# The fill of a tile of ones put first in a hand-ordered S4 + SwiGLU kernel, with a later planned start

## The chip, the cores and the metric

The kernel runs on one core of one Trainium2 chip. The metric is device time in microseconds (us) of one execution; smaller is better.

## The reference, cut to what matters

A layer norm feeds two branches, and their product is added to the input. L is 2048 rows, D 512 channels, N 128 states, F 1792.

```
x  = A_u                                   # 1 x 2048 x 512, float32
xn = layernorm(x)
P  = exp(dt * A * arange(L))               # complex, 512 x 128 x 2048
K  = real(einsum("dn,dnl,dn->dl", C, P, dt * B))
s  = causal_fft_convolution(xn, K) + xn * Dskip
g  = silu( (silu(xn @ w_gate) * (xn @ w_up)) @ w_down )
out = x + s * g
```

## The kernel before, in words

**What is computed where.** The feed-forward branch is done in float16 with a high and a low part of every operand, so that each product takes three matmuls (lines 699 and 741). The weights w_gate and w_up come in seven column chunks (g0 to g6, u0 to u6), each a load of 512 KB into a slot named wd. For each chunk ScalarE sums squares (line 604), VectorE copies the sums into hsq (line 614), one small TensorE matmul with a constant tile `ones` adds them over the partitions (line 615), VectorE makes the scale from that (lines 624 to 639), ScalarE writes the high part (line 669, L666 for u1 and later) and VectorE or GpSimd the low part (lines 670 and 667). The input rows x0 to x3 are loaded first (line 489), normed on VectorE and ScalarE (lines 503 to 531), transposed by TensorE (line 540) and copied back (line 546). Line 563 is the first stage of the convolution, whose results (line 567) are written to memory on SyncE's queue (line 568). Later come the convolution's kernel (lines 1070 to 1178), the products in frequency (1230 to 1287) and the output stage (1324 to 1340).

**What sets the order.** Every piece of work is a `Task` with an engine, a planned duration and its buffers. The string `LIST` (line 47) holds the order of all tasks, two characters for each; the first two tasks that the code adds, ids 0 and 1, are the fills

```
add("DVE", 0.2, lambda: (V.memset(ones, 2.0 ** -26), V.memset(halfpi, math.pi / 2)), up=[key("ones")], c=0)
add("POOL", 0.6, lambda: G.memset(dsk, 0.0), wr=[key("dsk")], c=0)
```

`ones` is read by line 615 and by the warming matmuls below; `halfpi` is read by ScalarE much later. Each engine issues its tasks in the order of the list. `Plan.run` walks through the list and gives every task a planned start and end, from its engine's free time, the ends of the tasks that it depends on plus a latency by engine (0.65 for PE, 0.35 for DVE and ACT), and a model of the transfers: `dma_free` is when the transfers planned so far are over, a transfer adds max(bytes / 280e3, pieces * 1.2e-3) us to it, and its data count as landed 1.9 us later. From the planned times come the PSUM bank of every task, the place of every buffer in the tile `arena` (`place`), extra waits that keep some VectorE and GpSimd work apart (`part_ports`), and the warming matmuls.

**The warming matmuls** (`keep_warm`, run at line 1423) are products of `ones` with itself into an unused bank; nobody reads them. For each planned gap of TensorE, from its end s of earlier work (1.5 for the first, `WARM_FROM`) to the planned start e of the next task, `keep_warm` puts

```
n = int((e - s - 0.2) * WARM_SHARE / WARM_DUR)      # 0.8 / 0.213
```

of them ahead of that task, if enough of the surrounding 3.4 us is idle in the plan. They do not alter the planned times of the tasks.

**Around the start**, the order on VectorE in the list before is: statistics of x1 and x0, the newton steps of their norm (lines 509 to 517), the hsq copy of g0, the fill of `ones` and `halfpi`, the low part of x0 (line 531), the scale of g0. The first TensorE task is the line 615 matmul of g0, with the first group of warming matmuls ahead of it.

Of the kernel before, what the change touches and what calls it, by code (L numbers as in the profile page):

```python
# [20 lines left out]
P = 128  # L21
L = 2048
D = 512
N = 128
# [20 lines left out]

DIGITS = "".join(chr(c) for c in range(35, 126) if c != 92)
LIST = (
    "#)#(#'#K#&#%#J#L#.#T#i#M#N#k###l#/#O#U#R#j#m#V#n#1#v#P#2#Q#S#D#Y#4#W#-#X#Z#5#+#w#o#x#y#q#,#p#r#*&+#8#z(*#s#t&.(+"
    "#]&/(,(.#}$&#7#[$'$(${(/$)#C#d#;#{#^&0#|$#(0#e(4#_#`&E#f%S&3$*#g&,#a$+#h#b#c(-#:$$(1$-#<&5$w&v(5$2&:&8$x(6$z$y$,"
    "#>$1$3$|$.(7&=#9%#$/(:(;$4$}#=&;#A(@&x$5$6$<%%%.$7&4$=$>(L$8(<%&(M&A$?$@$k$H$G$I(F(2#@(N$;%$(3&9#?$C&1&u#B$9(=&F"  # L50
    "%/(>%((H$D%2$J#0$K(?#6#3(G(I$:$A$S$R$T$N(O$L$B$t(A(R(S(B(J(K$E&6$F$O$](T$M(X(Z$q(P#E&J(C&@$%&?$Q(8(9(Q$0&y$P#u$U"
# [69 lines left out]
class Plan:  # L121
# [54 lines left out]

    def run(self):
        order = [self.tasks[i] for i in LIST]
        free = dict.fromkeys(("PE", "DVE", "ACT", "POOL", "SP"), 0.0)
        flight = {e: [] for e in free}  # L180
        banks = {k: [[None, 0.0] for _ in range(n)] for k, n in self.BANKS.items()}
        used, leaving, taken = 0, [], 0.0
        dma_free = port_free = 0.0
        shape = 0
        for at, t in enumerate(order):
            e, s = t.eng, free[t.eng]
            for d in t.deps:
                s = max(s, d.end + (0.0 if d.eng == e != "SP" else self.LAT[e]))
            for b in t.bufs:
                if b.over is not None:  # L190
                    continue
                b.over, b.first = 0.0, 2 * at
                if b.kind == "sb":
                    used += b.size
                    s = max(s, taken)
                    while used > ROOM and leaving:
                        x, n = heapq.heappop(leaving)
                        used -= n
                        s = max(s, x)
                    taken = s  # L200
                    continue
                best = None
                for k in b.kind:
                    for i, (held, x) in enumerate(banks[k]):
                        if held is None and (best is None or max(x, s) < best[0] - 1e-9):
                            best = max(x, s), k, i
                s, k, i = best
                b.at = k, i
                banks[k][i][0] = b
            if t.port:  # L210
                s = max(s, port_free)
            x = s + t.dur
            if e == "PE" and t.f32 != shape:
                x += SWITCH
                shape = t.f32
            t.start, free[e] = s, x
            if t.port:
                port_free = x
            if t.dma:
                dma_free = max(dma_free, x) + t.dma  # L220
                x = dma_free + 1.9
                flight[e].append(x)
                if len(flight[e]) >= 8:
                    free[e] = max(free[e], flight[e][-8])
            t.end = x
            for b in t.bufs:
                b.over = max(b.over, x)
                b.left -= 1
                if b.first == 2 * at:
                    b.since = round(s * 1e4)  # L230
                if not b.left:
                    b.till, b.last = round((b.over + REUSE) * 1e4), 2 * at + 1
                    if b.kind == "sb":
                        heapq.heappush(leaving, (b.over + REUSE, b.size))
                    else:
                        banks[b.at[0]][b.at[1]] = [None, b.over + REUSE]
        self.span = max(t.end for t in order)
        self.part_ports(order)
        order = self.keep_warm(order)
        self.place([b for b in dict.fromkeys(b for t in order for b in t.bufs) if b.kind == "sb"])  # L240
        return order
# [1229 lines left out]
```

## Time and profile before

| | |
|---|---|
| median of 3 runs | 613.95 us (611.83, 613.95, 614.11) |
| the profiled execution | 610.76 us, of which the span from the first to the last instruction is 609.0 |
| busy: PE, DVE, ACT, POOL | 581.9, 432.3, 342.1, 326.2 us |
| transfers | 93.10 MB, mean 153 GB/s |
| mean granted TensorE clock | 0.987 |
| warming matmuls | 44, all in the first 27 us |

Times in the views are us from the start of the span. In the timeline a row is start, duration, engine, line, operation, tiles, and in brackets the idle time of the engine before it and what ended that; neighbouring rows of one kind are merged with a count. PE is TensorE's matmuls, PEld its weight loads, DVE VectorE, ACT ScalarE, POOL GpSimd, SP SyncE; SPq is SyncE's queue, which issues most transfers. p names any PSUM bank, and arena any buffer of the arena.

### The profile page before, as it was taken

Reading aid. Unit: us, or ns where it says so; the run is one execution under the profiler, and the core shown is the slowest. Engines: PE = TensorE matmul, PEld = TensorE weight load, DVE = VectorE, ACT = ScalarE, POOL = GpSimd, SP = SyncE. Lnnn points to the kernel's source line nnn. Section 1 sums busy time; section 2 is a strip of 40 time slices with the busy share of each in tenths; the row PEclk is TensorE's granted clock in tenths of the full one; section 3 lists DMA queues with packets and bytes.
Section 4 is the critical chain, followed back from the end, with each engine's and each line's share of the span. In section 5 each row is a group of like instructions: output and inputs, shape, how many; then the busy total and the mean of one; then the engine's idle time right before and its main releaser. Section 6 shows DMA issues by size and latency. Waiting matters only on the chain.

```text
span 609.0 us, 18323 instructions
## 1 busy us (share of the span) xinstructions
PE 581.9 (96%) x7625; PEld 411.6 (68%) x7625; DVE 432.3 (71%) x988; ACT 342.1 (56%) x697; POOL 326.2 (54%) x301
## 2 busy tenths in 40 slices
PE   4999999999999999999999999999989999999974
PEld 1678886556888678766787677776657656667531
DVE  3777989665798989888779876878848556673313
ACT  5689856655765468667778687746632423131100
POOL 0145522279974768649997799688023341530131
PEclk9999999999999999999999999999989999999978
DMA  8699621024004041025340123556969889999997
GB/s 261 167 286 321 196 79 48 1 97 155 16 3 95 4 113 37 2 68 169 114 110 15 30 79 138 172 129 172 320 180 275 265 246 270 270 286 255 222 265 184
DMA packets 100594, 93.10 MB, mean 153 GB/s; under 512 B 38496, under 2 KB 83808, under 8 KB 100512
## 3 DMA queue, kind: packets, MB, share of 16 engines
q1 hardware_dynamic: 96000, 87.48, 50.0%
q10 hardware_dynamic: 4512, 4.46, 2.8%
q8 instruction: 60, 0.98, 0.7%
q14 instruction: 22, 0.18, 0.1%
HBM read 59.02 MB, written 32.90 MB: 151 GB/s over the span
## 4 chain that ended last, share of the span: by engine, by line
PE 84%; DMA 9%; DVE 3%; issue 1%; ACT 1%; SPq 0%; ACTq 0%; POOL 0%; DVEq 0%; POOLq 0%
PE p L699 45%; PE p L741 21%; PE p L1145 5%; DMA out_dram<-arena 3%; PE p L1230 3%; PE p L1237 2%; DMA arena<-zg_d 2%; DMA arena<-in_A_u_dram 2%; PE p L1277 2%; PE p L563 2%; PE p L1423 2%; PE p L1178 1%; DMA arena<-bs_d 1%; PE p L540 1%; DMA wd<-in_B_w_gate_dram 1%
## 5 line engine op out<-in xcount | busy, mean ns | idle before, releaser
L699 PE MATMUL p<-arena,wu 128*128 128x256 f16 x1344 | 157.3, 274 | 4.0 <-issue 4.0
L741 PE MATMUL p<-wd,arena 128*128 128x512 f16 x672 | 155.4, 381 | 0.0
L699 PE MATMUL p<-arena,wg 128*128 128x256 f16 x1344 | 155.2, 273 | 0.0
L699 PEld LDWEIGHTS <-wu 128*128 128x128 f16 x1344 | 130.7, 98 | 26.9 <-issue 8.8
L699 PEld LDWEIGHTS <-wg 128*128 128x128 f16 x1344 | 129.7, 98 | 23.0 <-issue 3.7
L741 PEld LDWEIGHTS <-arena 128*128 128x128 f16 x672 | 63.5, 98 | 77.1 <-issue 9.3
L1078 POOL TENSOR_TENSOR arena<-arena 128x1536 f32<-128x1536 f32 x32 | 90.7, 2840 | 18.0 <-DVE arena L854 5.6
L720 ACT ACTIVATE arena<-p,inv 128x512 f32<-128x512 f32 x56 | 38.4, 689 | 65.4 <-PE p L699 57.1
L1070 POOL TENSOR_TENSOR arena<-arena 128x1024 int32<-128x1024 int32 x32 | 62.4, 1955 | 18.5 <-DVE arena L830 7.5
L722 DVE SCALAR_TENSOR_TENSOR p<-p,shc,arena 128x512 f32<-128x512 f32 x56 | 42.2, 754 | 30.1 <-PE p L699 17.8
L724 ACT CAST arena<-p 128x512 f16<-128x512 f32 x56 | 32.5, 589 | 33.8 <-DVE p L722 16.4
L1113 DVE TENSOR_TENSOR arena<-arena,p 128x512 f32<-128x512 f32 x64 | 43.6, 681 | 8.4 <-ACT p L1094 6.4
L1336 POOL TENSOR_TENSOR arena<-arena 128x512 f32<-128x512 f32 x12 | 15.1, 1268 | 57.7 <-DMA arena<-in_A_u_dram 37.9
L725 DVE TENSOR_TENSOR arena<-p,arena 128x512 f16<-128x512 f32 x56 | 37.7, 683 | 11.2 <-ACT arena L724 11.2
L1094 ACT ACTIVATE p<-p,halfpi 128x512 f32<-128x512 f32 x64 | 42.4, 664 | 1.4
L1093 ACT ACTIVATE p<-arena 128x512 f32<-128x512 int32 x64 | 38.9, 610 | 6.4 <-DVE arena L1185 2.2
L1095 ACT ACTIVATE p<-arena 128x512 f32<-128x512 int32 x64 | 37.5, 602 | 8.7 <-DVE arena L1115 4.5
L1259 POOL TENSOR_TENSOR arena<-arena 128x512 f32<-128x512 f32 x16 | 20.3, 1275 | 38.5 <-DVE arena L1255 14.1
L1260 POOL TENSOR_TENSOR arena<-arena 128x512 f32<-128x512 f32 x16 | 20.3, 1272 | 31.3 <-DVE arena L1255 17.8
L1119 DVE SCALAR_TENSOR_TENSOR arena<-arena,p 128x256 f32<-128x256 f32 x64 | 26.5, 414 | 12.6 <-ACT p L1095 8.9
L1145 PEld LDWEIGHTS p<-arena 128*32 128x32 f32 x2048 | 29.7, 110 | 6.6 <-issue 4.2
L1145 PE MATMUL p<-arena 128*32 128x64 f32 x2048 | 33.4, 220 | 0.0
(180 smaller groups left out, 814.0 us busy)
## 6 DMA issues: line engine op xcount, KB each, us to landing
ax_d<-arena SPq DMA_DIRECT2D x32, 256.0 KB, 2.6
ak_d<-arena SPq DMA_DIRECT2D x16, 512.0 KB, 6.5
arena<-ak_d SPq DMA_DIRECT2D x16, 512.0 KB, 5.7
arena<-ax_d SPq DMA_DIRECT2D x16, 512.0 KB, 6.7
bs_d<-arena SPq DMA_DIRECT2D x32, 256.0 KB, 4.8
arena<-in_A_u_dram SPq DMA_DIRECT2D x62, 128.0 KB, 5.0
arena<-in_B_w_down_dram SPq DMA_DIRECT2D x14, 512.0 KB, 6.0
arena<-bs_d SPq DMA_DIRECT2D x14, 512.0 KB, 8.5
```

What stands on the lines that cost most here:

```text
L699: T.matmul(pg.t[:, i * 256:(i + 1) * 256].rearrange("p (a t) -> p a t", a=2), w[:, wl, d, i * P:(i + 1) * P], x[:, :, xl, d, :], start=(k ...
L720: add("ACT", 0.69, lambda: S.activation(sg.f32(), pg.t, AF.Silu, scale=inv[:, c, 0:1]), rd=[pg], wr=[sg], c=1, pr=e)
L722: add("DVE", 0.75, lambda: V.scalar_tensor_tensor(pu.t, pu.t, shc[:, c:c + 1], sg.f32(), op0=ALU.mult, op1=ALU.mult), rd=[sg], wr=[pu], c= ...
L725: add("DVE", 0.7, lambda: V.tensor_tensor(hh.view(F16)[:, 512:1024], pu.t, hh.view(F16)[:, 0:512], op=ALU.subtract), rd=[pu], wr=[hh], c=1 ...
L741: T.matmul(z.t, h[:, hl, i * 256 + t * P:i * 256 + (t + 1) * P], w[:, wl, i], start=(c == 0 and i == 0 and k == 0), stop=(c == NC - 1 and ...
L1070: G.tensor_tensor(a, h_[:, :, :, None].to_broadcast([P, 2 * GT, 4, 8]), l_[:, :, None, :].to_broadcast([P, 2 * GT, 4, 8]), op=ALU.add)
L1078: G.tensor_tensor(e, p_[:, :, :, None].to_broadcast([P, 3 * GT, 4, 8]), q_[:, :, None, :].to_broadcast([P, 3 * GT, 4, 8]), op=ALU.mult)
L1093: add("ACT", 0.62, lambda: S.activation(tc_.t, a(), AF.Abs, scale=SIN_SCALE), rd=[an], wr=[tc_], pr=pr)
L1094: add("ACT", 0.7, lambda: S.activation(tc_.t, tc_.t, AF.Sin, bias=halfpi, scale=-1.0), rd=[key("ones")], wr=[tc_], c=4, pr=pr)
L1095: add("ACT", 0.62, lambda: S.activation(ts.t, a(), AF.Sin, scale=SIN_SCALE), rd=[an], wr=[ts], pr=pr + 0.2)
L1113: V.tensor_tensor(o[:, :, 0:64].rearrange("p d (s j) -> p d s j", s=2), e[:, :, 0:64].rearrange("p d (s j) -> p d s j", s=2), t[:, :, None ...
L1145: T.matmul(kt[h * 32:(h + 1) * 32, (r * GD + dd) // 4], o[:, ri, dd + h, 64:96], o[:, ri, dd + h, 0:64], start=(ri == 0), stop=(ri == 1), ...
```

## The change: what it does

Three edits. In `LIST` the two characters of task 0 move from the fifteenth place (behind `#k`, the hsq copy of g0) to the first. In `Plan.run` the engines are planned to be free at 0.7 and no longer at 0, and the transfers at 1.2 and no longer at 0. The code of the tasks is the same.

```diff
 LIST = (
-    "#)#(#'#K#&#%#J#L#.#T#i#M#N#k###l#/#O#U#R#j#m#V#n#1#v#P#2#Q#S#D#Y#4#W#-#X#Z#5#+#w#o#x#y#q#,#p#r#*&+#8#z(*#s#t&.(+"
+    "###)#(#'#K#&#%#J#L#.#T#i#M#N#k#l#/#O#U#R#j#m#V#n#1#v#P#2#Q#S#D#Y#4#W#-#X#Z#5#+#w#o#x#y#q#,#p#r#*&+#8#z(*#s#t&.(+"
...
     def run(self):
         order = [self.tasks[i] for i in LIST]
-        free = dict.fromkeys(("PE", "DVE", "ACT", "POOL", "SP"), 0.0)
+        free = dict.fromkeys(("PE", "DVE", "ACT", "POOL", "SP"), 0.7)
...
-        dma_free = port_free = 0.0
+        dma_free, port_free = 1.2, 0.0
```

## The prediction

> **What bounds the kernel now.** I read the page first, then the busy time of each engine by stretches, then the timeline of the stretch in which TensorE isn't yet full, and last the chain of waits there. The page:
>
> ```profile
> span 609.0 us, 18323 instructions
> ...
> PE 581.9 (96%) x7625; PEld 411.6 (68%) x7625; DVE 432.3 (71%) x988; ACT 342.1 (56%) x697; POOL 326.2 (54%) x301
> ```
>
> TensorE is busy for 581.9 of 609.0 us. The stretches (busy time of each engine, then clock, share of the transfer engines, GB/s) show where the other 27 us lie, and where a gain at one end can pass through:
>
> ```profile
> 18.00:22.50 4.50, 4.50 (x42) 2.72 (x41) 4.00 (x14) 2.41 (x4) 0.00 (x0) 1.00 0.15 43
> 22.50:35.00 12.50, 11.41 (x107) 8.40 (x105) 10.12 (x30) 11.69 (x17) 5.84 (x3) 1.00 0.87 243
> 35.00:440.00 405.00, 405.00 (x5367) 299.66 (x5375) 327.63 (x761) 279.99 (x582) 270.09 (x255) 1.00 0.36 107
> 440.00:541.00 101.00, 97.05 (x1682) 65.24 (x1662) 60.58 (x115) 30.97 (x66) 36.42 (x30) 0.98 0.88 251
> 541.00:609.00 68.00, 55.01 (x420) 31.98 (x415) 24.70 (x48) 8.32 (x18) 13.67 (x11) 0.91 0.94 244
> ```
>
> From 35 to 440 TensorE has no idle time at all (405.00 of 405): what comes to it at 35 leaves it at 440, so whatever is gained ahead of 35 is handed on whole, unless a new wait arises. From 440 on, transfers are nearly full (0.88, 0.94). The stretch that the change touches is the first. Its timeline:
>
> ```profile
> 0.74 0.41 SPq L468 DMA_DIRECT2D idh_t<-in_idh_dram  x1
> ...
> 4.68 0.69 DVE L503 BATCH_NORM_STATS2 st<-arena 128x6 f32<-128x512 f32 x1 [4.68 <-DMA arena<-in_A_u_dram]
> ...
> 8.76 0.16 DVE L614 CAST hsq<-ssq 128x1 bf16<-128x1 f32 x1
> ...
> 8.89 0.17 DVE L474 MEMSET ones<- 128x128 bf16 x1
> ...
> 9.00 0.06 DVE L474 MEMSET halfpi<- 128x1 f32 x1
> ...
> 9.11 8.10 PE L1423 MATMUL p<-ones 128*128 128x512 bf16 x27 [9.11 <-DVE halfpi L474]
> ...
> 13.35 3.37 PEld L1423 LDWEIGHTS <-ones 128*128 128x128 bf16 x16 [0.28 <-issue]
> ...
> 17.05 0.17 PE L615 MATMUL p<-hsq,ones 128*128 128x1 bf16 x1
> ...
> 17.26 0.16 DVE L635 TENSOR_SCALAR ssq<-p 128x1 f32<-128x1 f32 x1 [6.38 <-PE p L615]
> ```
>
> This is the fault in the order. The sums of g0 are ready at 8.76 + 0.16 = 8.92. The matmul that needs them, line 615, runs at 17.05, because 27 warming matmuls stand ahead of it and none can begin before `ones` is filled. The plan has them from 1.5 on; they ran from 9.11. VectorE then idles for 6.38.
>
> **The change part by part.**
>
> *The fill.* Two instructions, 0.17 and 0.06 us. At their old place their 0.2 us are followed by a wait of VectorE for ScalarE (line 531, below), so taking them out gains nothing by itself. At the new place they run while VectorE has nothing to do until 4.68. The first issue of a queue is at 0.74; I take the fill at 0.75 and the first warming matmul 0.22 later, as now (8.89 to 9.11): 0.97.
>
> *The number of warming matmuls.* It follows from the formula of the planner. Planned before: the transfers of x1 and x0 begin at 0.6, four of 131072 / 280e3 = 0.468 each, then g0's of 1.872, and 1.9 until landed: 6.245. Latency 0.35, square 1.06, latency 0.35, hsq copy 0.16: 8.165. The fill ends at 8.365, plus 0.65 is e = 9.015; (9.015 − 1.5 − 0.2) × 0.8 / 0.213 = 27.5, so 27, as the row has. The later start moves the first transfer's end from 0.4 + 0.154 to 1.2 + 0.154; before, x1's transfer waited for its issue at 0.6, now for that, so everything that hangs on data moves by 0.754. The hsq copy ends at 8.919, no fill behind it: e = 9.569, 29.5, so 29. The next planned gap begins 0.2 earlier relative to its end: 5.6 becomes 6.3, so 6 in place of 5. All other gaps move as they are. So 44 become 47. At 3.37 / 16 = 0.21 us each the three cost 0.6 us of TensorE.
>
> *The rest of the plan.* Past the first few tasks all planned times move by the same 0.754. Bank choice, arena places and the pairs kept apart rest on differences of planned times, so they stay. Only the first line 615 matmul (+0.55), the fill and the first issues (+0.70) differ, and none of these shares a bank or a place with an earlier task. No cost, then, if this holds; it is the slower rival if not.
>
> *The group of warming matmuls, early.* 8.10 + 2 × 0.21 = 8.5 us from 0.97 on: over at 9.5. Line 615 for g0 then runs at 9.5 and not at 17.05, 7.5 us earlier. That is not the gain, since its readers have other waits:
>
> ```profile
> 10.12 0.75 DVE L531 SCALAR_TENSOR_TENSOR arena<-arena,rstd 128x512 f16<-128x512 f32 x1 [1.06 <-ACT arena L530]
> ...
> 13.21 1.06 ACT L604 ACTIVATE wu<-wd 128x1024 bf16<-128x1024 f32 x1 [0.43 <-DMA wd<-in_B_w_up_dram]
> ...
> 14.17 0.19 ACT L604 ACTIVATION_READ_ACCUMULATOR wu<-wd 128x1 f32 x1
> ...
> 17.64 1.15 ACT L669 ACTIVATE wg<-wd,scw 128x1024 f16<-128x1024 f32 x1 [3.28 <-DVE scw L624]
> ...
> 17.72 0.13 DVE L639 TENSOR_SCALAR shc<-scw 128x1 f32<-128x1 f32 x1
> ...
> 20.87 1.15 ACT L669 ACTIVATE wu<-wd,scw 128x1024 f16<-128x1024 f32 x1 [2.09 <-DVE scw L624]
> ...
> 20.89 1.28 DVE L670 SCALAR_TENSOR_TENSOR wg<-wd,scw,wg 128x1024 f16<-128x1024 f32 x1
> ...
> 22.62 1.27 DVE L670 SCALAR_TENSOR_TENSOR wu<-wd,scw,wu 128x1024 f16<-128x1024 f32 x1
> ```
>
> VectorE: line 531 ends at 10.87, and the scale of g0 (17.26 to 17.85, 0.6 us) runs behind it, to 11.5. So line 615 may be as late as 10.7 and costs nothing; the two more warming matmuls lie inside that. ScalarE: ahead of the high part of g0 in its order stands the square of u1, whose load lands at 13.2 whatever the order; with its readout it ends at 14.36. So the high part starts at 14.36 and not at 17.64: 3.28 gained, no more. The high part of u0 waited another 2.09 for its scale. That scale comes behind the hsq copy of g1 and u1, which needs the same 14.36, and is done at about 15.1, while ScalarE is on g0 until 15.5. So that wait goes too: 3.28 + 2.09 = 5.37. VectorE's line 670 for g0 starts when the high part is there, 15.55 and not 20.89: 5.34. From there on VectorE runs without a gap in the chain of waits, and that chain goes over ScalarE to the last wait of TensorE ahead of its full stretch:
>
> ```profile
> 20.89 1.28 DVE wg L670
> ...
> 22.63 1.27 DVE wu L670
> ...
> 32.13 1.28 ACT L720
> ...
> 34.17 0.82 PE p L563 x6
> ...
> 34.99 5.35 PE p L699 x48
> ```
>
> TensorE on the way has these rows now:
>
> ```profile
> 17.08 1.24 PE L1423 MATMUL p<-ones 128*128 128x512 bf16 x5
> ...
> 20.82 0.17 PE L615 MATMUL p<-hsq,ones 128*128 128x2 bf16 x1
> ...
> 21.67 2.58 PE L699 MATMUL p<-arena,wg 128*128 128x256 f16 x22
> ```
>
> From the first line 615 to the first line 699 it takes 21.67 − 17.05 = 4.6 us; from 9.5 on that would be 14.1, but the line 615 of g1 and u1 needs sums of 14.36 and their copy (0.2 with the handover, and 0.2 more to TensorE), so it runs at 14.8, and line 699 0.85 later, as now: 15.65, 6.0 earlier. Then TensorE waits for the low part of g0 (15.55 + 1.28 = 16.8), so its lead falls back to VectorE's 5.3. The sixth warming matmul of the second group (0.2) lies in the wait until 14.8. If there were no such covers, the three would cost their 0.6. I take 0.1 off for handovers: **5.2 us** at 34.17, between 3.28 (ScalarE's first wait alone) and 7.5 (all of line 615).
>
> *The queue.* The next load, g3, stands behind the write of line 568 (a row of the queue's waits, one of the stretches, two of the timeline, and one of the issues, whose last column is the median time to landing):
>
> ```profile
> SPq L568 <- ACT arena L567: 8.9, 1, 8.9
> ...
> 21.00:22.50 1.50, 1.50 (x14) 0.88 (x15) 1.43 (x4) 1.50 (x3) 0.00 (x0) 1.00 0.00 0
> ...
> 22.97 0.38 SPq L468 DMA_DIRECT2D wd<-in_B_w_gate_dram  x1
> ...
> 36.09 1.07 ACT L604 ACTIVATE wg<-wd 128x1024 bf16<-128x1024 f32 x1
> ...
> wd<-in_B_w_gate_dram SPq DMA_DIRECT2D x7, 512.0 KB, 5.1
> ```
>
> The queue waits 8.9 for line 567, which follows TensorE's line 563; with that some 5 earlier g3 is issued near 17.8. The transfer engines, which run dry in the stretch 18.00 to 22.50 (share 0.15, at its end 0.00), have 0.85 × 4.5 = 3.8 us of that to win. So the transfers come 3.8 earlier where the engines come 5.2 earlier. What covers the difference: g3, issued at 22.97 and landed some 5.1 later, isn't read until 36.09, 8 us of room.
>
> *After 34.17.* TensorE's 405 us without a gap shift whole. Past 440 the transfers are full, but they begin with what the engines have written, so I let them shift too.
>
> **Sum.** 610.76 (609.0 and 1.76 around it) − 5.2 = 605.6 for an execution like the profiled one. That one was 3.2 us below the median of the runs shown; against the median it is 613.95 − 5.2 = **608.7**.
>
> **Rivals.**
>
> *Transfers bound the stretch from 22 to 35.* Their share there is 0.87. Then only their 3.8 counts: 610.1. Against it speaks the room of 8 us for g3. Chance 0.10, mostly still faster.
>
> *Only ScalarE's first wait goes* (u0's scale is late again, or x2 and x3 land after 18.5 and hold VectorE's chain): 3.28, 610.7. Chance 0.05.
>
> *TensorE's clock falls back.* The first warming matmuls are slow, the later ones twice as fast:
>
> ```profile
> 12.93 0.15 PEld L1423 LDWEIGHTS <-ones 128*128 128x128 bf16 x1 [0.28 <-issue]
> ```
>
> A weight load each 0.15 + 0.28 = 0.43 up to 13.35, then 0.21: some ten slow ones, 10 × 0.22 = 2.2 us. If TensorE idled long between 9.5 and 15.65, these 2.2 would be paid a second time on real work: 5.2 − 2.2 = 3.0, 610.9. It decides only if the idle time is one long piece; by the rows above the work between the two is 4.6 of 6.2 us, and the 1.6 left is split over several waits. Chance 0.04. The Trainium skill, "TensorE: Matmul & The Clock Gate", section "Part 1: The HAM clock gate", says that the array goes back to half its clock after an idle window of about 3.4 us, and that the number of slow matmuls at the start varies from run to run; this speaks against moving the warming away from the work. The trace agrees on the ratio (0.43 to 0.21 us), while its clock column reads 1.00 in these stretches; no row of it shows a fall back.
>
> *The gain is lost in the last 170 us.* Transfers at 0.88 and 0.94 set the end, and if they did not begin earlier, nothing would be left: 613.5. Against it: between 440 and 541 their queue stands and waits for VectorE's part of TensorE's work,
>
> ```profile
> SPq L1193 <- DVE arena L725: 9.8, 1, 9.8
> ```
>
> which shifts. Chance 0.08.
>
> *Slower: buffers come to lie elsewhere.* If planned times do not move evenly, the arena is laid out anew, and a load of the last stretch can fall on a place whose reader is late. Such a hold is worth what the queue's row just above shows, 9.8; where the transfers have no spare share it passes to the end: 613.95 − 5.2 + 9.8 = 618.5. Slower by more than 0.5% from a hold of 8.3 on. Against it: the shift of 0.754 by hand is even past the first loads. Chance 0.07.
>
> That the fill does not run early (VectorE not ready at 0.75) would not matter until 2.2: the group of 8.5 would then end at 10.7. Larger gains, up to 7.5 (606.4), get 0.02.
>
> **How the numbers follow.** Forecast (about 5.2) 0.64; transfers 0.10; ScalarE 0.05; clock 0.04; lost at the end 0.08; slower 0.07; larger 0.02. 0.5% is 3.07 us, about what a measurement of this kernel can tell from no change. Faster by more: 0.64 + 0.02 + 0.08 of the transfers' + 0.03 of ScalarE's = 0.77; slower 0.07; the rest, 0.16, within. The range: the largest gain gives 606.4, and single runs before lay up to 2.1 under the median, so I go to 605.0 below; above, it takes in transfers, ScalarE and clock with 1 us of spread, 612.0, and leaves out the end and the slower case, 0.15.
>
> **What would show it.** Right: line 474 near 0.8; the first warming matmul near 1.0, 47 in all, 29 in the first group; line 615 near 9.5; no wait of line 635 over 2 us; line 669 for g0 at 14.4 directly behind the square of u1, and for u0 directly behind it; line 670 at 15.6; the first line 699 at 15.7; g3 issued near 17.8; line 563 ahead of the full stretch near 29; TensorE full from there to about 435. Wrong: a first group that still ends past 10.9; a gap at line 669 for u0; idle TensorE between 30 and 435; or waits of the queue that the trace of before doesn't have.

## The result, and the profile after

| | median | runs |
|---|---|---|
| before | 613.64 us (611.12 to 615.97) | 19 |
| changed | 611.43 us (606.31 to 616.07) | 19 |

The ratio is 0.9954, 95% interval 0.9934 to 0.9975, which is 0.46% less; by the medians it is 2.2 us less, where 5.2 were forecast. Two later sets of 12 runs gave 0.9955 (0.9927 to 0.9984) and 0.9941 (0.9912 to 0.9970). The profiled execution took 612.37 us. (Two of the 19 runs of the changed kernel were over 1.5% slower than its fastest and are left out of the ratio, not of the median.)

The page of the changed kernel:

```profile
span 610.6 us, 18328 instructions
...
PE 583.4 (96%) x7628; PEld 411.7 (67%) x7628; DVE 432.6 (71%) x988; ACT 342.0 (56%) x697; POOL 326.7 (54%) x301
```

This span is longer than the 609.0 of before, although the median is lower. One profile of each is not enough here, and where the time goes must be read stretch by stretch. The start, in the timeline of the changed kernel:

```profile
0.83 0.17 DVE L474 MEMSET ones<- 128x128 bf16 x1 [0.83 <-PEq L1456]
...
1.05 8.24 PE L1423 MATMUL p<-ones 128*128 128x512 bf16 x29 [1.05 <-DVE halfpi L474]
...
8.72 1.06 ACT L604 ACTIVATE wg<-wd 128x1024 bf16<-128x1024 f32 x1 [2.40 <-DMA wd<-in_B_w_gate_dram]
...
10.11 0.16 PE L615 MATMUL p<-hsq,ones 128*128 128x1 bf16 x1 [0.82 <-DVE hsq L614]
...
14.87 1.13 ACT L669 ACTIVATE wg<-wd,scw 128x1024 f16<-128x1024 f32 x1
...
16.04 1.28 DVE L670 SCALAR_TENSOR_TENSOR wg<-wd,scw,wg 128x1024 f16<-128x1024 f32 x1 [0.42 <-ACT wg L669]
...
17.98 0.38 SPq L468 DMA_DIRECT2D wd<-in_B_w_gate_dram  x1
...
19.39 0.69 DVE L503 BATCH_NORM_STATS2 st<-arena 128x6 f32<-128x512 f32 x1 [0.35 <-DMA arena<-in_A_u_dram]
...
29.52 0.82 PE L563 MATMUL p<-arena,f1x_t 64*128 64x512 f16 x6 [1.27 <-ACT arena L720]
```

The fill runs at 0.83, the first group from 1.05 to 9.3, and line 615 no longer waits for it but for its data. TensorE's last wait ahead of its full stretch ends at 29.52 and no longer at 34.17: 4.65 us gained.

Then the gain is lost again. The waits of TensorE from 15 to 541 us in the changed kernel (for whom, total, times, longest; "issue" is time in which it waited for nothing that the profile shows):

```profile
PE p L1237 <- issue: 5.8, 2, 5.3
PE p L563 <- ACT arena L724: 1.3, 1, 1.3
...
PE p L699 <- issue: 0.7, 1, 0.7
PE p L1145 <- issue: 0.7, 1, 0.7
...
```

The same view of the kernel before, from 100 to 541:

```profile
PE p L699 <- issue: 4.0, 2, 2.7
```

The large one in each timeline, changed kernel first, then before:

```profile
437.61 1.06 PE L1237 MATMUL p<-arena 64*32 64x256 f32 x30
444.00 1.06 PE L1237 MATMUL p<-arena 64*32 64x256 f32 x2 [5.33 <-issue]
```

```profile
441.06 0.28 PE L699 MATMUL p<-arena,wu 128*128 128x256 f16 x1
...
444.01 4.07 PE L699 MATMUL p<-arena,wu 128*128 128x256 f16 x23 [2.67 <-issue]
```

In the changed kernel TensorE stops after 30 of 32 equal matmuls whose data are there. That is no wait for work.

### The profile page after: what moved, and what is told of

It reads as the page before. It is cut to its first block, busy times and chain, and to the rows that moved or that the text cites. A ratio compares the mean times of both kernels' runs of the same rounds, so it can differ in the third digit from the quotient of the medians.

```text
span 610.6 us, 18328 instructions
## 1 busy us (share of the span) xinstructions
PE 583.4 (96%) x7628; PEld 411.7 (67%) x7628; DVE 432.6 (71%) x988; ACT 342.0 (56%) x697; POOL 326.7 (54%) x301
## 3 DMA queue, kind: packets, MB, share of 16 engines
q10 hardware_dynamic: 4512, 4.46, 2.8%
## 4 chain that ended last, share of the span: by engine, by line
PE 87%; DMA 5%; issue 2%; ACT 2%; SPq 2%; DVE 1%; ACTq 0%; DVEq 0%
PE p L699 47%; PE p L741 22%; PE p L1145 5%; DMA arena<-bs_d 3%; PE p L1237 3%; PE p L1230 2%; PE p L1277 2%; PE p L1324 2%; PE p L563 2%; PE p L1178 1%; DMA arena<-in_A_u_dram 1%; SPq L468 1%; DMA out_dram<-arena 1%; PE p L540 1%; SPq L489 1%
```

## What the stop is

TensorE's instructions have a transfer queue of their own. The queues of the kernel before, and the changed kernel's in the two microseconds 441 to 443 of the stop:

```profile
q8 instruction: 60, 0.98, 0.7%
```

```profile
q1 hardware_dynamic: 738, 0.74, 106.1%
q8 instruction: 1, 0.02, 2.8%
```

0.98 MB in 60 packets is 16 KB each. TensorE has 2 × 7625 matmuls and weight loads; with the 95 semaphore and drain instructions of its sequencer the trace has 15,345, and 60 × 256 is 15,360: I take a packet to be a read of 256 instructions of TensorE. I counted from the traces how many of the 15,345 had begun when each read started. In quiet stretches the read number n (from 0) starts when about 256 n + 160 have begun. At the read that ends the stop near 440 it is 256 n + 449, the same 449 in the first profile of each kernel and in eight others. TensorE had used up what it held; the read, between loads that fill the transfer engines, came late: at 441.3 before, at 441.5 in the changed kernel, where TensorE had run dry at 438.67.

The other stops are of the same kind. From 40 to 541 us the 14 traces have 42 stops of TensorE over 0.15 us. Forty of them, the one of 1.3 near 352 that the view above puts down to ScalarE among them, come when exactly 256 k + 193 instructions have begun (449 is 256 + 193), and TensorE goes on 1.2 to 1.6 us after the end of a read; the other two stand ahead of line 1324.

The length adds up, too. In the kernel before, the 289 instructions from 256 n + 160 to 256 n + 449 take 3.53 us at the stop near 441 (9.8 in the median of all traces). The read began 3.52 us after the first of them, where 1.1 is the median in this trace; it took 1.17, and TensorE went on 1.50 after its end: 3.52 + 1.17 + 1.50 − 3.53 = 2.66. With the median 1.1 this sum gives a stop of some 0.2, an estimate. So it takes both, a burst of small matmuls and a late read. Over all traces a read begins 0.9 us after 256 n + 160 in the median where the transfer engines are less than 0.3 busy in the microsecond that follows (417 reads), and 2.8 us after it where they are over 0.9 busy (255 reads); the read itself takes 1.0 to 1.1 in both.

The Trainium skill, "Runtime: NRT & Kernel Launch", section "Instruction fetch mechanics", says that instructions are refilled in blocks of 16 KB, 256 instructions, over a DMA queue of the sequencer's own; the packets agree. It also says that this is hidden, since instructions are dispatched more slowly than they are filled. Here it isn't: 2.67 and 5.33 us.

The stop has a second price, in the stretches of the kernel before (the column before the last two is the granted clock):

```profile
442.00:444.00 2.00, 0.00 (x0) 0.00 (x0) 1.70 (x3) 0.00 (x0) 0.15 (x1) 0.87 1.00 347
444.00:446.00 2.00, 1.99 (x10) 1.40 (x11) 0.00 (x0) 0.00 (x0) 2.00 (x2) 0.50 1.10 375
446.00:448.00 2.00, 2.00 (x15) 1.43 (x13) 0.00 (x0) 0.00 (x0) 0.33 (x1) 0.78 0.64 203
```

After it TensorE runs at 0.50 of its clock. The rival of the falling clock had the right mechanism at the wrong place.

## The experiments

The table gathers all profiles. "Earlier" is how much earlier an instruction of VectorE starts than the same one (by its place in VectorE's order, which past the first 10 us is the same in all) in the first profile of before, taken at 340, 432, 452 and 541 us of that one. "Warming" counts the matmuls that nobody reads, small ones too.

| kernel | warming | ratio (95%) | earlier at 340 | 432 | 452 | 541 |
|---|---|---|---|---|---|---|
| before | 44 | 1 | 0 | 0 | 0 | 0 |
| before again | 44 | 0.9995 (0.9968 to 1.0023) | −1.90 | −3.16 | −4.50 | −3.97 |
| times alone | 47 | 1.003 (1.000 to 1.006) | −1.38 | −1.61 | −3.40 | −2.97 |
| before + 64 | 108 | 0.9940 (0.9913 to 0.9967) | −1.13 | −1.34 | 0.98 | 1.58 |
| changed | 47 | 0.9954 (0.9934 to 0.9975) | 4.64 | 3.32 | −1.38 | −2.45 |
| changed again | 47 | 0.9955 (0.9927 to 0.9984) | 3.82 | 3.30 | 1.80 | 1.58 |
| changed, third | 47 | 0.9941 (0.9912 to 0.9970) | 4.42 | 4.46 | 2.18 | 2.97 |
| list alone | 44 | 0.9940 (0.9913 to 0.9967) | 5.21 | 3.23 | 3.55 | 3.45 |
| list alone, again | 44 | 0.9934 (0.9907 to 0.9961) | 4.41 | 4.46 | 3.40 | 2.96 |
| changed + 64 | 111 | 0.9865 (0.9829 to 0.9901) | 4.67 | 4.71 | 7.34 | 7.49 |
| changed + 96 | 143 | 0.9849 (0.9813 to 0.9884) | 4.71 | 2.97 | 4.91 | 6.35 |
| changed + 128 | 175 | 0.9952 (0.9929 to 0.9975) | 3.94 | 3.16 | 1.71 | 1.09 |
| before, half loads | 44 | 0.9916 (0.9884 to 0.9949) | −0.32 | −0.51 | 0.87 | 2.26 |
| changed, half loads | 47 | 0.9930 (0.9892 to 0.9968) | 4.16 | 4.03 | 3.88 | 5.16 |

**The changed kernel once more.**

> The changed kernel once more. Theory: TensorE is full from about 29.5 as in the first profile (4.65 earlier than before); later it stops a few times with nothing to wait for, while 16 KB instruction reads come late behind the loads of the last stretch. These stops are luck of the execution: their sum past 100 us differs by some us from the first profile's, and the time is 0.990 to 0.999 of before. Rival (the loss is a fixed part of the changed program): the same stops at the same places, 1.3 at 352 and 5.3 at 439.

The median was 610.91 beside 614.0 of before. The start gained 3.82, and the stops were others than in the first profile: 0.47 near 352, 3.41 near 438. So their size is luck in part, but they stand at the same places, as the rival has it.

**The list alone.** The fill moved, the planned times left at 0.

```diff
-        free = dict.fromkeys(("PE", "DVE", "ACT", "POOL", "SP"), 0.7)
+        free = dict.fromkeys(("PE", "DVE", "ACT", "POOL", "SP"), 0.0)
...
-        dma_free, port_free = 1.2, 0.0
+        dma_free = port_free = 0.0
```

> Fill first, planned times as before: 44 warming matmuls, 26 in the first group and 6 in the second. Theory (the fill's place alone makes the gain): line 615 for g0 at about 10, TensorE full from 29.4 to 29.7, as in the changed kernel. If the loss past 35 is luck: 0.990 to 0.999 of before. If it hangs on where TensorE's 256-instruction reads fall in its program (here as in the kernel before, by the count of 44): less is lost than in the changed kernel, 0.991 to 0.994, 4.7 us. Rival (the later planned times make the gain): TensorE full only from 34, ratio 1.000.

609.14 beside 614.0. Its program is the changed kernel's without three warming matmuls, and it has the whole start (5.21). Of the three edits the fill's place makes the gain. It too stopped near 440, for 3.2 us on line 699, and its 0.9940 lies in both ranges of the expectation, so this run alone doesn't tell luck from the places of the reads.

**The times alone.** The list of before, the later planned times.

> Fill at its old place, planned times as in the changed kernel: 47 warming matmuls, 30 in the first group and 5 in the second. Theory: the first group runs from 9.1 to 17.8, three matmuls longer than before, so TensorE is full from 34.8, 0.6 later: ratio 1.000 to 1.002, and if the reads' places matter, up to 1.005. Rival (the planned times make the gain): 0.995.

615.04 beside 614.0. The first group of 30 begins only at 9.99 in this profile; the start is 1.38 later than the first profile of before, 0.5 later than the mean of the other kernels with the late fill, where 0.6 was expected. The later times by themselves gain nothing. Whether they lose is not clear: the interval of the ratio reaches down to 1.000.

**64 more matmuls.** The first group of the changed kernel has 10 warming matmuls as they are and 83 small ones.

```diff
-            for i in range(n):
+            for i in range(n + (64 if s == WARM_FROM else 0)):
...
+            return lambda: T.matmul(bank_t[at[0]][at[1]][:, 0:64], ones, ones[:, 0:64], start=True, stop=True)
```

> The changed kernel with the first group made of 10 warming matmuls as they are and 83 small ones (64 columns), so 64 more in all: every 16 KB read of TensorE's instructions falls 128 instructions, half a read, earlier in the program. Line 615 may be up to 1 us later, TensorE full from 29.5 to 30.5. Theory that the places of the reads matter: the stops near 352 and 439 change by over 2 us, either way, beyond what the two profiles of the changed kernel differ by, and the median moves by 2 or more. Theory that they are luck: median within 1 us of the changed kernel's, plus what line 615 is late.

605.13 beside 614.0, 8.9 us less, and 5.8 less than the changed kernel beside it, with the same start (4.67). Its waits of TensorE from 100 to 541, all of them:

```profile
PE p L1145 <- issue: 1.5, 1, 1.5
PE p L1237 <- issue: 0.8, 1, 0.8
```

In place of one long stop there are two short ones, at other instructions; nothing near 352. The median moved by more than the 2 us that the theory of the reads' places asked for.

**The same shift without the early start.** 64 small matmuls of the identity tile, which is there early, ahead of the first group of the kernel before.

```diff
+            return lambda: T.matmul(bank_t[at[0]][at[1]][:, 0:64], idh_t, idh_t[:, 0:64], start=True, stop=True)
```

> The kernel before, with 64 small matmuls of the identity tile (64 columns, into the unused bank) put first on TensorE, where it idles until 9.1 anyway. The fill stays late, so the start gains nothing: TensorE full from 34.0 to 34.9 as before. Theory (where the 16 KB reads of TensorE's instructions fall sets how long it stands still near 440, whatever the start does): the stop of 2.7 near 441 gets shorter or splits, the clock stays up, and the time is 0.992 to 0.997 of before. Rival (the half-read shift helps only together with an early start, or the better time of the shifted kernel came from its small warming matmuls): 0.999 to 1.001.

609.82 beside 613.51, with a late start (−1.13). The shift of the reads alone is worth as much as the whole change, and its waits from 100 to 541 show why:

```profile
PE p L1230 <- issue: 1.6, 1, 1.6
PE p L1237 <- issue: 0.4, 1, 0.4
```

**96 more, and 128 more.** The second is the one that decides, since 128 matmuls and their weight loads are 256 instructions, one read.

> The changed kernel with 96 more matmuls in the first group (10 as they are and 115 small ones of 64 columns), so the reads fall 192 instructions, three quarters of a read, earlier in the program. The group ends by 9.5, so the start is as in the changed kernel: TensorE full from 29 to 30.5. If the places of the reads matter: stops near 352 and 439 unlike those of the changed kernel and of the one with 64 more, and a time between 0.985 and 1.002 of before, not the 0.9955 of the changed kernel. If any more small matmuls do it: as with 64 more, 0.9865.

> The changed kernel with 128 more matmuls in the first group (10 as they are and 147 small ones), so the reads of TensorE's instructions fall 256 instructions, exactly one read, earlier: at the same places of the program as in the changed kernel. The start: TensorE full from 29 to 30.5. Theory (the places of the reads set what is lost later): the gain of the shifted kernels goes away again, 0.993 to 0.998 of before, with one stop of 3 to 5 near 438. Rival (many small matmuls early are what helps): 0.985, as with 96 more.

604.31 beside 613.51, and 610.01 beside 612.95. Three quarters of a read give 0.9849, which fits more small matmuls as well; its stops from 100 to 541 are of 1.6 and 1.2, at other instructions again. A whole read gives the changed kernel's ratio again, although it has the most small matmuls. Its largest stop is the old one, behind the same 30 of 32 matmuls and with the same 449:

```profile
436.94 1.06 PE L1237 MATMUL p<-arena 64*32 64x256 f32 x30
441.41 0.84 PE L1237 MATMUL p<-arena 64*32 64x256 f32 x2 [3.41 <-issue]
```

So what counts is where the reads fall in TensorE's program, and the small matmuls as such don't. Both shifted kernels beat the changed one.

**Half the loads.** The loads ahead of lines 1230 and 1237 bring half of their bytes; what the other half would have replaced stays, so only the time of these two kernels counts.

```diff
-            load(lambda b=b: b.f32().rearrange("p (q d) -> p q d", q=4), src[:, :, c * 256:(c + 1) * 256], [b],
+            load(lambda b=b: b.f32().rearrange("p (q d) -> p q d", q=4)[:, 0:2], src[:, 0:2, c * 256:(c + 1) * 256], [b],
```

> The kernel before with the loads of the products in frequency halved: each of the 32 loads of 512 KB brings only the first two of its four blocks, the rest of the buffer keeps what lay there. Theory (instruction reads are late because the loads fill the transfer engines): no stop of TensorE over 1 us without a waited-for instruction between 300 and 540, its clock not below 0.95 there, and the time is 0.985 to 0.995 of before, also because the last stretch has less to move. Rival (the stops have another cause): the stop near 441 stays at 2 or more.

> The changed kernel with the same halved loads. Theory: no stop over 1 us between 300 and 540, so the gain of the start is kept whole: 3.8 to 5.2 us less than the kernel before with halved loads, in the profiles at 540 and in the medians. Rival (the lost gain goes elsewhere, such as the last writes): 2.2 less in the medians although no stop is there.

608.74 and 607.90 beside 613.51. The expectation fell: the stop is still there, 2.66 in the first and 2.04 in the second. Up to 541 the changed kernel keeps 2.9 of 4.5 over the other, and by the medians 0.8, with wide intervals. At the stop itself the transfer engines were still full with half the bytes, so this did not take the suspected cause away: the read began 3.89 and 3.01 us after 256 n + 160, about as late as the 3.52 of before. That full transfer engines are what makes a read late thus rests on the comparison over all reads above, and no run here removes the load to test it.

**The third profile, the list again, before against itself.**

> The changed kernel a third time, on the chip of the run of the list's edit alone: 0.993 to 0.998 of before, with stops near 352 (0.4 to 1.3) and 438 (3 to 5.5).

> The edit of the list alone once more: the changed kernel's program without three warming matmuls. Theory (six instructions of shift matter): 1 to 2 us less than the changed kernel beside it. Rival (luck): within 0.7 us of it.

> The kernel before against itself: 0.998 to 1.002. Its profile shows how far the start and the stops differ between executions of one program: TensorE full from 34 to 35.5, a stop near 441 of 2.5 to 4.

609.54, 608.88 and 612.83 beside 612.95. The third profile of the changed kernel has the stop near 438 (3.4), but none near 352, where one was expected. The list alone was 0.7 under the changed kernel, which is the rival's figure (luck) and not the 1 to 2 of the theory; in the earlier set it was 1.8. The sign is the same, each is within the intervals, and whether six instructions of shift cost time isn't settled by it. Before against itself shows how far executions differ: its last wait ahead of the full stretch ended at 35.91 (34 to 35.5 was expected), its start was 1.90 later than in the first profile, and its stop near 445 took 3.5:

```profile
PE p L699 <- issue: 4.2, 2, 3.5
```

## Why the prediction was right or wrong

**The start was right.** Point by point: the fill (0.83), the first group (1.05), 29, 6 and 47, line 615 (10.11, forecast 9.5), the high part of g0 behind the square of u1 (14.87, 14.4), line 670 (16.04, 15.6), the first line 699 (16.07, 15.7), g3 (17.98, 17.8), line 563 (29.52, 29). The 0.2 to 0.6 by which these are late came from the load of g0, read at 8.72 and no longer at 7.58, after which ScalarE has hardly a gap; later a load of input rows held VectorE for 0.35. So late loads cost a few tenths, the first of them ahead of the stretch from 22 to 35 that the rival of the transfers named. Forecast 5.2, first pair 4.65. But the first profile of before started early: nine profiles with the early fill stand at 4.44 in the mean at 340, four with the late one (times alone left out) at −0.84. The difference is 5.3.

**The step that failed is "TensorE's 405 us without a gap shift whole", and with it "past 440 ... I let them shift too".** Everything behind 35 did shift whole up to 340: 4.65, 4.63 and 4.64 us at 50, 140 and 340 in the first pair. Then TensorE ran dry, first for 1.28 us at 352, which is the "idle TensorE between 30 and 435" that the prediction named as a sign of being wrong. Such stops were in the profile of before ("issue: 4.0, 2, 2.7"): its stretch 440 to 541 had only 97.05 of 101 busy; I quoted that stretch and passed over the missing 4 us. A stop without a reason is a reason to look at the instructions.

**The three added warming matmuls were priced at nothing, or 0.6 without cover. What they cost, far from their place, is not settled.** They move every read six instructions earlier in the program, so that the stop near 440 falls on line 1237 (with 47) and not on line 699 (with 44). From 432 to 452 the four profiles with 44 lose 0, 1.34, −0.32 and 1.06, in the mean 0.5; the five whose reads fall as with 47 (175 among them) lose 4.70, 1.50, 2.28, 1.46 and 1.79, in the mean 2.3. The two sets don't overlap, but 0.12 is all that parts them, and the stretch was picked afterwards: from 340 to 541 the four lose 0, 2.07, 1.76 and 1.45, the five 7.09, 2.24, 1.45, 2.85 and 1.59, and there they overlap. The medians point the same way: the changed kernel gained 2.2, 3.1 and 3.4 in its three sets, the list alone 4.9 and 4.1. None of this is clear of the noise. So of a start worth 5.3 some 2 to 3 us were lost again. The profiles show where: from 340 to 541, the stretch of the stops, the three of the changed kernel lose 3.6 in the mean, the two of before 1.0. How much of that is the shift by three matmuls, and how much differs from run to run, stays open.

**The other rivals.** Slower by another layout of the buffers: the two programs differ only in the fill and the three matmuls, so the even shift of the plan held. Lost in the last 170 us: in effect 2 to 3 of 5 us were, but not by the mechanism named there. The falling clock: the prediction says that no row of the trace shows a fall back, but its own rows of 440 to 541 and 541 to 609 read 0.98 and 0.91. The range (605 to 612) held the time by luck: it was drawn for rivals of the start, and the start gained what was forecast. Of the chances, 0.77 went to faster by over 0.5%, and 0.46% is within.

## What to carry to other kernels

A gain at the start of a full engine is worth what reaches the end, so follow one engine's instructions through both traces and see where their lead changes. Read "issue" gaps of a full engine as instructions that aren't there: count the engine's instructions, its sequencer's included, against the packets of its instruction queue, see whether the stops come at one place of a block, and look for bursts of tiny matmuls beside large loads. There a few dummy instructions at an idle start can be worth more than the edit under study: here the changed kernel with 96 more took 604.31 beside 613.51 us, and without them it gained 2.2 to 3.4.

## What the runs showed of the hardware that was not expected

TensorE holds few instructions ahead: the read numbered n starts in quiet stretches when 256 n + 160 instructions have begun, and must be there when 256 n + 449 have. All stops but two from 40 to 541 us, 40 in 14 profiles, come at that place; near 440 TensorE stood still there for 2.66 to 5.33 us in ten profiles, with data and banks ready.

A stop of 2.67 us was followed by a granted clock of 0.50. The Trainium skill, "TensorE: Matmul & The Clock Gate", section "Part 1: The HAM clock gate", names an idle window of about 3.4 us for that; the shorter stop here did it too. But the length of the stop doesn't decide alone: in the changed kernel with half loads the clock fell after 2.04 us, and in the kernel before with half loads it stayed at 1.00 through a stop of 2.66, as in the list alone through one of 3.2. The two kernels with half loads, before first:

```profile
440.00:480.00 40.00, 37.33 (x655) 27.09 (x640) 26.45 (x52) 12.21 (x28) 15.04 (x12) 1.00 0.57 169
```

```profile
440.00:480.00 40.00, 40.00 (x690) 29.03 (x695) 24.83 (x49) 12.70 (x28) 13.74 (x11) 0.96 0.54 157
```
